# Strassen's algorithm for six more first-layer chunks, and a table that says which engine copies and adds

## The chip, the cores and the metric

The kernel runs on one core of one Trainium2 chip. The metric is device time in microseconds (us) for one execution; lower is better. Everything is float32, apart from the two weight matrices, which arrive as 64-bit floats and are turned into float32 on the chip. The core's engines are TensorE (PE in the profile; PEld is its loading of stationary operands), VectorE (DVE), ScalarE (ACT), GpSimd (POOL) and SyncE (SP, which only issues DMAs here).

## The reference

Eight batches of 512 tokens, each with eight heads of 64, read from and write to 32 state rows per head; the joined rows then go through a two-layer network with the ELU function between. Cut to what matters:

```python
scores = x @ state.T * scale;  a  = softmax(scores);  xread = a  @ state   # (8, 8, 512, 64)
scores2 = state @ x.T * scale; a2 = softmax(scores2); sread = a2 @ x       # (8, 8, 32, 64)
x = concat([xread, sread], axis=2)  ->  (8 * 544, 512)
h = x @ w_in                                       # (4352, 2048)
g = where(h > 0, h, exp(min(h, 0)) - 1)
out = g @ w_out                                    # (4352, 512)
```

## The kernel before, in words

**The first layer without its input.** For the 512 tokens of a batch, `x @ w_in` is `a @ (state @ w_in)`. So the kernel makes M = state @ w_in per batch (256 rows of heads and states, 2048 columns; `make_m`, L757), and the first layer is M.T @ a.T, with 256 as the length of the sum. M is made in eight pieces of 256 columns (hc 0 to 7), and a *chunk* c (0 to 3) is two pieces, 512 of the 2048 hidden columns. The state rows of all batches go through `states` (L1656) at the end.

**Two ways to do a chunk.** Batches 2 to 7 use `ffn1_chunk` (L1013): Strassen's algorithm in Winograd's form, which multiplies 2x2 blocks with seven products in place of eight. Its left sums s1, s2, s3, s4 of M come from `sum_m` (L846, four operations of 256 columns on GpSimd), its right sums t1 to t4 of a from `sum_a` (L855, four of 256 on VectorE). Three copies carry partial sums between PSUM banks, two additions with a PSUM operand finish the blocks, and `elu` (L963) turns each of the four blocks of 512 columns into g. Batches 0 and 1 use `ffn1_plain` (L982): per chunk four tiles, each two matmuls with a moving operand of 512 columns, and `elu`. An `elu` is Exp on ScalarE, then either Relu on ScalarE and one VectorE operation, or two VectorE operations.

**Order of stages.** `start` (L1302) loads x, the states and sixteen weight blocks of 1 MB each (three raw buffers, so block n+3 can be loaded only when block n has been converted). `convert` (L1255) is two ScalarE operations and four VectorE operations per block, the last of them an exact 32-bit integer addition that shows in the profile as CUSTOM_DVE_ANT_0. Blocks 0 to 7 are w_in, 8 to 15 w_out. In between it makes a and M of batches 0 and 1 and does their eight chunks; then follows their second layer (also Strassen, `Strassen` L1202 and `Second` L1067, whose sums are VectorE operations of 512 or 1024 columns). `batch` (L1573) then does batches 2 to 7, each prepared while the one before it is in its second layer.

**What sets the order.** No engine's order follows the program text. The kernel is written as 2,832 numbered operations; `Plan.add` (L290) finds their dependencies, and `ORDERS` (L50) holds for each engine the list of operation numbers in the order in which it issues them. `Plan.follow` (L364) walks these lists with a table of costs (for VectorE and GpSimd it takes a shared port as held by one of them at a time: `port`, L541 to L575) only to interleave the program and place 40 us of filling matmuls (`fill`, L1728) where TensorE would wait at the start. On the chip each engine runs its list strictly in order and waits on semaphores. SyncE's list sets the order of the loads. All engine instructions are issued from one helper, so the profile names them all L532.

Of the kernel before, what the change touches and what calls it, by code (L numbers as in the profile page):

```python
# [22 lines left out]
    "load_w": (0.46, 325e3), "load_x": (0.55, 297e3, 0.2), "load_states": (0.6, 180e3, 0.2),  # L23
    "load_blocks": (0.66, 280e3, 2.1), "move_state": (0.66, 280e3, 0.6),
# [16 lines left out]
def in_order(text):  # L41

    ops = []
    for part in text.split():
# [4 lines left out]

ORDERS = {  # L50
    PE: in_order(
        "26 23 16 29 89 92 201 19 203 95 69 59 66 205 81 85 127 63 62 138 134 217 215 130 112 116 157 142 146 178 "
        "160 171 182 186 190 174 248 245 226 230 259 262 219 222 234 266 278 270 282 305 308 320 317 286 290 324 "
        "410 411 423 294 442 443 336 274 332 424 412 348 444 340 413 425 414 445 446 426 352 328 427 344 428 415 "
        "447 416 417 451 452 448 453 429 430 480-482 491-494 483 449 495 484-486 500 487 496-498 528 454-456 "
        "529-532 541 533 534 542 623 535 543 544 550-552 545 457 553 546 554 458 555 547 548 556 557 628 571 570 "
        "629 619 573 574 639 620 621 640 625 641 643 645 648 649 665 662 663 685 609 670 671 667 682 683 693 687 "
        "661 694 697 709 743 706 707 746 712 681 780 747 752 767 754 745 783 784 759 808 789 782 812 811 791 796 "
        "817 832 810 819 835 836 824 841 834 887 843 848 864 870 860 903 871-873 892 893 884 885 883 900 901 889 "
        "989 905 908 973 899 909 978 970 979 971 986 975 969 987 1007 994 991 995 1035 1004 985 1005 1023 1009 "  # L60
        "1012 1013 1073 1020 1031 1003 1032 1021 1044 1025 1045 1019 1050 1076 1077 1097 1047 1082 1075 1110 1084 "
        "1089 1113 1114 1138 1119 1112 1141 1142 1121 1126 1147 1162 1140 1149 1165 1166 1154 1171 1164 1217 1173 "
        "1178 1194 1200 1190 1201 1319 1222 1223 1202 1230 1203 1213-1215 1231 1219 1233 1235 1238 1239 1229 1300 "
        "1301 1303 1305 1308 1309 1353 1316 1317 1299 1321 1337 1324 1325 1333 1315 1334 1335 1342 1343 1339 1350 "
        "1351 1403 1355 1365 1361 1362 1406 1407 1374 1375 1440 1380 1349 1377 1412 1405 1443 1414 1419 1444 1427 "
        "1449 1442 1468 1451 1456 1472 1471 1492 1470 1477 1495 1496 1479 1501 1484 1494 1503 1520 1508 1547 1649 "
        "1563 1532 1533 1552 1544 1545 1553 1549 1524 1530 1531 1543 1560 1568 1561 1569 1565 1630 1559 1633 1631 "
        "1638 1635 1639 1629 1654 1646 1655 1647 1664 1651 1695 1667 1645 1665 1733 1683 1669 1672 1673 1663 1691 "
        "1680 1692 1681 1679 1685 1770 1704 1705 1737 1710 1736 1707 1742 1735 1774 1773 1749 1744 1779 1757 1772 "
        "1798 1781 1786 1822 1801 1800 1802 1807 1825 1826 1809 1831 1814 1824 1833 1850 1877 1838 1854 1860 1862 "  # L70
        "1861 1863 1873 1874 1882 1875 1883 1893 1890 1891 1879 1889 1895 1898 1963 1899 1975 1968 1960 1969 1961 "
        "1976 1979 1965 1977 1959 1981 1984 2025 1985 1997 1994 1993 1995 2002 1999 2013 2003 2021 2010 2022 2011 "
        "2034 2015 2035 2063 2040 2009 2066 2087 2037 2100 2072 2067 2103 2074 2065 2104 2109 2079 2128 2102 2111 "
        "2152 2116 2131 2132 2155 2137 2156 2161 2139 2130 2163 2154 2180 2144 2168 2207 2192 2193 2191 2204 2205 "
        "2203 2212 2209 2213 2223 2220 2190 2184 2221 2219 2225 2228 2289 2293 2229 2298 2290 2299 2291 2306 2309 "
        "2295 2307 2327 2314 2311 2315 2305 2324 2343 2325 2355 2329 2379 2332 2323 2333 2351 2340 2352 2416 2341 "
        "2339 2364 2345 2365 2381 2370 2383 2382 2367 2388 2419 2420 2390 2395 2425 2403 2427 2418 2440 2442 2432 "
        "2443 2464 2444 2449 2467 2468 2451 2473 2456 2466 2513 2475 2480 2492 2494 2546 2562 2498 2509 2499 2518 "
        "2510 2519 2511 2529 2515 2497 2526 2525 2534 2527 2535 2531 2543 2542 2544 2558 2548 2551 2637 2552 2567 "
        "2559 2568 2560 2580 2564 2577 2596 2578 2585 2582 2667 2586 2604 2593 2665 2594 2605 2598 2608 2576 2635 "  # L80
        "2609 2592 2611 2639 2638 2669 2644 2668 2646 2674 2694 2676 2651 2750 2698 2681 2697 2751 2722 2703 2725 "
        "2696 2731 2724 2733 2705 2752 2759 2726 2753 2710 2754 2755 2760 2738 2756 2782 2757 2761 2762 2771 2763 "
        "2772 2764 2783 2784 2773 2774 2765 2775 2785 2776 2786 2777 2778 2787 2766 2792 2793 2788 2794 2795 2789 "
        "2796-2799 2812 2822 2813 2814 2802-2805 2815 2806-2809 2823 2824 2816-2819 2825-2829 "
    ),
    DVE: in_order(
        "28 25 18 48 30-32 54 36 195 194 35 50 49 55 39 56 51 57 41 21 42 44 43 200 122 45 123 97 124 96 125 102 "
        "98 84 208 209 105 101 152 107 110 108 111 109 154 153 88 155 168 115 166 137 167 169 145 119 240 242 141 "
        "241 243 181 185 149 256 254 255 214 257 300 193 477 302 301 189 229 303 312-315 225 358 360 269 233 237 "
        "359 478 365 361 281 366 273 367 368 537 289 285 372 374 373 297 375 386-389 327 379 419 335 381 380 382 "  # L90
        "277 395 420 393 339 407 394 405 406 293 396 351 408 399 434 421 343 331 401 400 436 422 716 720 476 438 "
        "402 435 479 437 439 538 355 440 432 441 489 502 501 507 433 503 490 347 518 517 562 506 717 510 512 516 "
        "539 431 536 514 603 576 652 582 655 578 579 565 586 583-585 540 604 632 581 549 563 580 566 577 567 633 "
        "653 564 636 631 568 459 569 656 606 654 637 638 626 657 635 627 674 658 646 651 723 659 675 678 647 634 "
        "523 679 718 660 680 673 668 676 719 677 669 721 688 690 689 696 691 605 713 714 750 751 722 755 758 762 "
        "807 763 787 788 765 792 806 766 815 799 816 800 795 858 802 820 803 804 879 823 828 840 805 844 827 831 "
        "881 852 851 847 856 857 877 875 876 917 878 855 859 933 922 880 897 882 916 895 913 896 918 891 906 932 "
        "907 914 982 898 925 911 915 981 921 998 927 983 976 977 931 929 984 912 943 992 961 944 997 999-1001 963 "
        "1002 938 993 962 1016 1010 1017 1015 964 1018 1011 1034 1026-1029 1051 1052 1080 1081 1085 1093 1088 "
        "1095 1117 1118 1096 1136 1092 1122 1137 1145 1146 1130 1125 1129 1188 1132 1133 1150 1135 1209 1153 1158 "  # L100
        "1170 1174 1157 1161 1134 1182 1177 1186 1205 1185 1206 1207 1246 1187 1208 1181 1210 1211 1189 1212 1227 "
        "1225 1247 1226 1243 1228 1252 1262 1248 1241 1263 1221 1255 1236 1244 1245 1312 1328 1251 1311 1242 1313 "
        "1257 1329 1306 1307 1322 1330 1259 1314 1268 1327 1331 1261 1291 1273 1274 1293 1323 1332 1237 1345 1346 "
        "1340 1292 1341 1348 1347 1356-1358 1294 1364 1359 1381 1382 1410 1411 1415 1422 1423 1425 1447 1418 1426 "
        "1448 1452 1459 1460 1455 1475 1462 1476 1463 1518 1539 1480 1541 1500 1488 1483 1504 1465 1487 1507 1512 "
        "1516 1517 1535 1491 1536 1467 1519 1466 1511 1515 1464 1540 1537 1542 1538 1555 1557 1556 1573 1551 1577 "
        "1576 1558 1575 1592 1582 1593 1566 1574 1642 1572 1643 1571 1636 1641 1578 1644 1637 1567 1585 1658 1581 "
        "1657 1587 1652 1653 1591 1589 1603 1604 1659-1661 1676 1670 1678 1677 1621 1662 1675 1622 1671 1598 1694 "
        "1624 1686-1689 1711 1712 1623 1740 1741 1745 1753 1752 1755 1756 1777 1778 1748 1797 1782 1790 1794 1785 "
        "1792 1789 1793 1795 1805 1848 1806 1869 1810 1796 1830 1813 1818 1867 1834 1817 1837 1821 1846 1847 1842 "  # L110
# [128 lines left out]
class Plan:  # L239
# [50 lines left out]
    def add(self, engine, cost, emit, ins, outs, port=False, moved=0, tokens=((), ()), name="", shape=None):  # L290
# [38 lines left out]
        for b in banks.values():  # L329
# [4 lines left out]
            b.last = op  # L334
        op.deps.discard(op)
        self.ops.append(op)
        return op

    def prepare(self):
        for op in self.ops:  # L340
# [114 lines left out]
def kernel(  # L455
# [340 lines left out]
    def copy_m(b, c, to):  # L796
        for g in range(G):
            A.copy(out=to[:, g * 512 : (g + 1) * 512], in_=st[b, "m", c][g])
# [974 lines left out]
```

## Time and profile before

| what | value |
|---|---|
| median of three runs (lowest, highest) | 688.26 us (687.98, 689.55) |
| the profiled execution: its time, its span | 688.75 us, 687.0 us |
| TensorE clock granted | full, in all 40 slices of the span |
| busy in the span: PE, DVE, ACT, POOL | 678.3, 568.5, 328.7, 110.2 us |
| TensorE: first matmul that is no filling, last matmul's end | 4.64 us, 683.3 us |
| start of the first matmul of batch 2's first layer | 186.07 us |

The page's first part gives busy time per engine, its second part the span in 40 slices of 17.2 us. Later views cut the span in stretches of one's own choice (busy time of each engine in each), group instructions by the tiles that they write and read and by shape (`out<-in`, count, busy time, mean ns of one), list who waited for whom, or show instructions in order of time. One float32 matmul of the program stands as two matmul records. A record's duration includes its way through the array and overlaps the next one, so the pace is read from a run of records in the timeline.

### The profile page before, as it was taken

To read this page: it belongs to the slowest core of one execution; us is meant where nothing else is said; L and a number is where in the kernel's file an instruction comes from. 1 tells how busy PE (TensorE), PEld (TensorE's weight loads), DVE (VectorE), ACT (ScalarE), POOL (GpSimd) and SP (SyncE) were. 2 spreads that over 40 slices of the span, in tenths; PEclk is the share of its full clock that TensorE was granted. 3 is DMA by queue.
4 is the path that set the end of the run, shared out by engine and by line. 5 is a ranking of instruction groups with operands and counts; after the bars stand their busy time and mean duration, and the time that the engine had idled before them with its cause. 6 is when DMAs were issued, how large, how long until landed. Compare 5 with 4: busy or idle time off the path is not lost.

```text
span 687.0 us, 15056 instructions
## 1 busy us (share of the span) xinstructions
PE 678.3 (99%) x6098; PEld 588.6 (86%) x6098; DVE 568.5 (83%) x896; ACT 328.7 (48%) x734; POOL 110.2 (16%) x133
## 2 busy tenths in 40 slices
PE   8999999999999999999999999999999999999997
PEld 7534568889988988899988998899889998999997
DVE  5999999989769993999569985998499966988661
ACT  5999972301266324833276316732484328611530
POOL 1100000200240124103230151112420333000000
PEclk9999999999999999999999999999999999999999
DMA  9899550007581046230573156213732040330401
GB/s 272 270 264 303 180 184 1 0 5 263 171 219 36 1 124 182 50 108 2 158 168 77 45 148 150 77 57 99 239 62 86 8 128 28 104 113 1 154 1 31
DMA packets 88457, 78.57 MB, mean 114 GB/s; under 512 B 56516, under 2 KB 69956, under 8 KB 88388
## 3 DMA queue, kind: packets, MB, share of 16 engines
q1 hardware_dynamic: 87844, 77.09, 38.4%
q8 instruction: 48, 0.79, 0.5%
q10 hardware_dynamic: 544, 0.52, 0.2%
q14 instruction: 21, 0.17, 0.1%
HBM read 59.77 MB, written 14.68 MB: 108 GB/s over the span
## 4 chain that ended last, share of the span: by engine, by line
PE 71%; issue 7%; ACT 6%; DMA 5%; DVE 5%; SPq 4%; POOL 1%; DVEq 0%; POOLq 0%
PE ps L532 71%; SPq L532 4%; ACT sec L532 3%; DMA xr<-in_state_dram 1%; DVE g L532 1%; POOL xr L532 1%; DMA o<-in_x_dram 1%; ACT t_w L532 1%; DVE xr L532 1%; DMA t_w<-in_moe_w_in_dram 1%; ACT w_half L532 1%; DMA m<-m_mem 1%; DVE sec L532 1%; DMA out_dram<-o 1%; ACT w_out L532 1%
## 5 line engine op out<-in xcount | busy, mean ns | idle before, releaser
L532 ACT COPY ps<-ps 128x128 f32<-128x128 f32 (+2 forms) x169 | 55.3, 332 | 227.6 <-PE ps L532 170.2
L532 PE MATMUL ps<-aT,m 128*128 128x256 f32 (+1 forms) x568 | 149.1, 406 | 1.1 <-DMA m<-m_mem 1.1
L532 PEld LDWEIGHTS ps<-aT,m 128*128 128x128 f32 x568 | 105.0, 190 | 29.4 <-issue 11.7
L532 PE MATMUL ps<-w_out,g 128*128 128x128 f32 (+1 forms) x768 | 115.4, 293 | 0.0
L532 PEld LDWEIGHTS ps<-w_out,g 128*128 128x128 f32 x768 | 102.1, 192 | 6.2 <-ACT m L532 1.7
L532 DVE TENSOR_TENSOR o<-o,ps 128x256 f32<-128x256 f32 (+2 forms) x108 | 55.9, 531 | 39.2 <-PE ps L532 34.3
L532 POOL TENSOR_TENSOR m<-m 128x256 f32<-128x256 f32 x72 | 56.9, 805 | 120.3 <-ACT m L532 103.9
L532 POOL TENSOR_TENSOR xr<-xr,small 128x512 f32<-128x512 f32 x24 | 31.0, 1305 | 278.0 <-PE ps L532 168.5
L532 PE MATMUL ps<-sec 128*128 128x128 f32 x560 | 72.9, 276 | 0.0
L532 PEld LDWEIGHTS ps<-sec 128*128 128x128 f32 x560 | 67.7, 192 | 1.0 <-issue 0.4
L532 PE MATMUL ps<-t_w,s 128*128 128x128 f32 (+1 forms) x432 | 67.9, 299 | 0.0
L532 ACT ACTIVATE xe<-ps 128x512 f32<-128x512 f32 x96 | 55.5, 597 | 14.4 <-PE ps L532 8.0
L532 PEld LDWEIGHTS ps<-t_w,s 128*128 128x128 f32 x432 | 59.0, 191 | 3.8 <-issue 0.8
L532 DVE SCALAR_TENSOR_TENSOR g<-xe,ps 128x512 f32<-128x512 f32 x66 | 43.9, 678 | 7.3 <-ACT xe L532 6.8
L532 DVE TENSOR_TENSOR ps<-sec,ps 128x512 f32<-128x512 f32 (+1 forms) x52 | 34.7, 668 | 9.7 <-PE ps L532 6.3
L532 ACT ACTIVATE xe<-xe 128x512 f32<-128x512 f32 x66 | 41.0, 633 | 1.1
L532 PE MATMUL ps<-aT,s 128*128 128x256 f32 x168 | 41.1, 379 | 0.2 <-DVE ps L532 0.2
L532 ACT COPY sec<-ps 128x512 f32<-128x512 f32 (+1 forms) x52 | 29.6, 569 | 21.2 <-PE ps L532 21.1
L532 ACT COPY m<-ps 128x256 f32<-128x256 f32 (+1 forms) x56 | 26.9, 497 | 26.6 <-PE ps L532 26.3
L532 PE MATMUL ps<-sec,g 128*128 128x128 f32 (+1 forms) x392 | 37.7, 259 | 1.2 <-DMA g<-in_x_dram 1.2
L532 PEld LDWEIGHTS ps<-sec,g 128*128 128x128 f32 (+1 forms) x392 | 34.7, 173 | 2.5 <-DMA g<-in_x_dram 1.7
L532 PE MATMUL ps<-w_out,sec 128*128 128x256 f32 (+1 forms) x176 | 36.6, 351 | 0.0
(149 smaller groups left out, 1158.0 us busy)
## 6 DMA issues: line engine op xcount, KB each, us to landing
w_half<-w_in_mem SPq DMA_DIRECT2D x48, 512.0 KB, 4.8
t_w<-in_moe_w_out_dram SPq DMA_DIRECT2D x8, 1024.0 KB, 5.6
t_w<-in_moe_w_in_dram SPq DMA_DIRECT2D x7, 1024.0 KB, 7.1
out_dram<-o SPq DMA_DIRECT2D x14, 512.0 KB, 4.2
xe<-in_x_dram SPq DMA_DIRECT2D x26, 256.0 KB, 3.2
o<-in_x_dram SPq DMA_DIRECT2D x80, 64.0 KB, 3.0
w_in_mem<-w_half SPq DMA_DIRECT2D x8, 512.0 KB, 3.8
xr<-xr SPq DMA_DIRECT2D x96, 32.0 KB, 3.0
```

Of the source, the lines that this page charges most:

```text
L532: ins = getattr(engine, name)(**named)
```

## The change

1. **Six chunks.** Chunks 1, 2 and 3 of batches 0 and 1 go through `ffn1_chunk`; chunk 0 of both stays plain. They get their own `sum_m` and, once per batch, `sum_a`; scratch space comes from buffers that are free at that time, and the third PSUM bank from the common pool.
2. **Places.** Copies, two-operand sums, the short scale operations and the middle step of `elu` go through `plan.pick`, which looks the operation's number up in a table `PLACES` of 110 entries; without an entry the engine is the one of before. Read with the numbering, the entries move, ahead of batch 2's first layer, 32 operations from DVE to POOL (ten additions of `convert`; seven `combine` halves of 1024 columns; seven sums of `sum_a` for batches 0 and 1; and some of 512 columns), 14 from POOL to DVE (13 of `sum_m`), 23 from ACT to DVE (13 of them copies of M of 256 columns) and 6 from DVE to ACT. From batch 2 on, 29 go from DVE to POOL and 6 others move.
3. **Orders.** All five lists are new. On SyncE the load of weight block 1 now stands ahead of batch 1's x; the states of batches 2 to 7 and block 2 follow. On TensorE the matmuls of batch 3's first chunk that stood six places (of 775) earlier against the work around them now come later.
4. **Costs in the table** for three kinds of DMA change and two are added; this moves only the plan's own times, not the orders, which are written out.

There are 2,912 operations after it: 775 on PE (757 before), 895 on DVE (896), 195 on POOL (126), 713 on ACT (719) and the same 334 on SP.

```diff
+    def pick(self, options, engine):
+        engine = PLACES.get(len(self.ops), engine)
+        options[engine]()
+        return engine
...
+    def both(out, in0, in1, op, engine=DVE):
+        plan.pick(
+            {
+                DVE: lambda: V.tensor_tensor(out=out, in0=in0, in1=in1, op=op),
+                POOL: lambda: Q.tensor_tensor(out=out, in0=in0, in1=in1, op=op),
+            },
+            engine,
+        )
...
-        V.tensor_tensor(out=bits, in0=bits, in1=q, op=ALU.add)
+        both(bits, bits, q, ALU.add)
...
-        pa, pc, pb = bank(), bank(), fixed[c % 2].view()
+        pa, pc, pb = bank(), bank(), bank() if b < 2 else fixed[c % 2].view()
+        u = ob[:, b * 1024 :] if b < 2 else sec[:, 7680 + c % 2 * 1024 :]
...
+        def ffn1_sums(b, c):
+            if (b, c) == (b, {0: 1, 1: 1}[b]):
+                sum_a((a_sb, s_buf)[b])
+            more = m1_more[c] if b else None
+            sum_m(g_of[b, c], more)
+            for part in ffn1_chunk(b, c, (g0, g_sb)[b], (a_sb, s_buf)[b], more):
+                part()
...
-            ffn1(0, c)
             if c < 2:
                 for b in range(2):
                     softmax_rows(b)
                     turn_state(b)
                     state_read(b, (x_halves, x_1)[b])
-            ffn1(1, c)
+            for b in range(2):
+                ffn1_sums(b, c)
```

## The prediction, made before the result was known

> **What bounds the kernel now.** I read four views in this order: the page's head, busy time by stage, TensorE's waits, and single stretches of the timeline.
>
> ```profile
> span 687.0 us, 15056 instructions
> PE 678.3 (99%) x6098; PEld 588.6 (86%) x6098; DVE 568.5 (83%) x896; ACT 328.7 (48%) x734; POOL 110.2 (16%) x133
> ```
>
> The stages (busy PE, PEld, DVE, ACT, POOL):
>
> ```profile
> 6.00:20.00 14.00, 12.32 (x300) 9.35 (x308) 12.25 (x24) 10.37 (x24) 2.16 (x2) 1.00 1.08 312
> 20.00:60.00 40.00, 39.65 (x493) 18.57 (x478) 37.50 (x54) 39.81 (x80) 2.06 (x2) 1.00 0.88 273
> 60.00:100.00 40.00, 39.77 (x181) 22.87 (x180) 39.23 (x49) 37.05 (x58) 0.00 (x0) 1.00 0.70 220
> 100.00:150.00 50.00, 50.00 (x238) 41.46 (x238) 45.69 (x57) 11.22 (x23) 4.96 (x4) 1.00 0.00 1
> 150.00:185.00 35.00, 35.00 (x332) 33.02 (x331) 34.69 (x59) 4.99 (x17) 1.82 (x3) 1.00 0.56 184
> ```
>
> TensorE's waits in the whole span:
>
> ```profile
> PE ps L532 <- DMA g<-in_x_dram: 1.2, 3, 0.7
> PE ps L532 <- DMA m<-m_mem: 1.1, 1, 1.1
> PE ps L532 <- ACT m L532: 0.5, 2, 0.3
> PE ps L532 <- DMA xr<-in_state_dram: 0.4, 1, 0.4
> ```
>
> A busy PE could still be a slow one, so the pace decides. From two runs of records:
>
> ```profile
> 70.89 3.70 PE L532 MATMUL ps<-s,g 128*128 128x512 f32 x8
> 87.32 1.89 PE L532 MATMUL ps<-w_out,sec 128*128 128x256 f32 x8
> ```
>
> Eight records of 512 columns take 3.70, and a single one stands with about 0.60 in the groups' mean, so they start every (3.70 - 0.60) / 7 = 0.44; where nothing waits, starts are 0.429 apart (0.10 of this run is its first record's). Likewise 256 columns start every 0.216. At these paces the gaps between full-size matmuls from 20 us to the end sum to some 9 us in 663, mostly pieces of 0.1 and less at changes of matmul shape; the largest is 1.3. So TensorE is the bound from 20 us to its last matmul at 683.3, and whatever leaves its list shortens the run, if the other engines still deliver in time. The stages show where that is doubtful: from 20 to 60 us DVE and ACT are at 94% and 99%, from 60 to 100 DVE at 98%, from 150 to 185 at 99%. The changed chunks lie between about 34 and 106 us.
>
> **TensorE's work: -4.9.** A plain chunk is 4 tiles x 2 matmuls x 2 records = 16 records of 512 columns, 16 x 0.429 = 6.86. By seven products it is 7 x 2 x 2 = 28 records of 256 columns, 28 x 0.216 = 6.05. The difference is 0.82; six chunks give 4.9. The weight loads (0.19 each) stay below 0.216 and hide.
>
> **What the chunks add elsewhere.** Per chunk: two PSUM additions on DVE (rows of 0.68 that start 0.61 apart), three PSUM copies of 0.58 (ACT), four sums of M of 256 columns; per batch four sums of a. That is 12 additions, 18 copies, 24 + 8 sums. The `elu` work has the same elements as before.
>
> **What the table moves, ahead of batch 2 (until 186 us).** DVE loses 32 operations to POOL and gets 14 from POOL, 23 from ACT (13 of 256 columns) and gives ACT 6. With starts 1.15 apart for 1024 columns, 0.61 for 512 and 0.35 for 256 I count, for operations that read two SBUF operands or run single-source in SBUF at double pace: before 54 x 1.15 + 30 x 0.61 + 56 x 0.61 + 8 x 0.35 = 117; after 38 x 1.15 + 30 x 0.61 + 49 x 0.61 + some 26 x 0.35 = 101. The other DVE operations grow from 94 to 124, about +15. DVE stays at 168 us, of some 175 (from 6 us to batch 2's start, 4 us earlier than now). ACT in its tight stage, 20 to 60, gives away nine copies and a few others and takes on the new PSUM copies of chunk 1: about 2.5 less, while TensorE saves 2 x 0.82 there. So the two tightest engines keep step. That is why I let the saving of TensorE stand. After batch 2's start DVE has 60 us of work in a batch of 83, so the 29 moves there I cost at nothing; what hides them is DVE's idle time (66.90 busy of 80 in 250 to 330); without it each would cost TensorE at most its extra length of some 0.4.
>
> **POOL's additions: +1.2.** POOL's rows:
>
> ```profile
> L532 POOL TENSOR_TENSOR m<-m 128x256 f32<-128x256 f32 x72 | 56.9, 805 | 120.3 <-ACT m L532 103.9 <-PE ps L532 9.9 <-DMA m<-m_mem 5.1
> L532 POOL TENSOR_TENSOR xr<-xr,small 128x512 f32<-128x512 f32 x24 | 31.0, 1305 | 278.0 <-PE ps L532 168.5 <-DVE small L532 78.3 <-issue 31.1
> ```
>
> Undisturbed ones take 0.72 (256) and 1.04 (512, one operand repeated). No row has 1024 columns or integers. From below, on the slope of these two: 0.72 + 3 x 0.32 = 1.7; from above, in proportion, 4 x 0.72 = 2.9. I take the middle, 2.3. As integers it might go as 2,048 half-words, as on DVE: 8 x 0.72 = 5.7, the far end. [...]
> DVE does the same addition in 1.15 steps, so a moved one comes 1.15 later. Four of them (blocks 1, 2, 3, 5) feed `make_m` from 20 to 60 us, and each is a new wait: PE's list is in order, so behind `make_m` stand all the ffn1 matmuls; behind the store of the block on SP stands the load of the next one. In the trace the time from the end of the last operation that feeds such a `make_m` to its start is 0.29, 0.23, 0.26 at three and about 2 at two. I charge one of four, 1.2. Ends: -0.7 (DVE earlier, TensorE's 0.7 of waits on M and the like gone) and +4.6 (all four).
>
> **Startup: +0.9.** With block 1 (1 MB) ahead of batch 1's x, x lands about 1 MB at 300 GB/s = 3.5 later than the 15.5 at which TensorE's last wait for it now ends, so near 19. By 19.95 TensorE now has behind it the state turns (0.7) and batch 1's scores (0.9) that it will then still owe, but it will have done 0.75 of `make_m`: 0.9 lost. Ends: 0 (filled by other work) and 1.6.
>
> **The fetch of M: -1.1.** TensorE waits 1.1 at 255.35 for a DMA issued at 249.74 behind SP's other issues. The new list uses it some six places (about 5 us) later. Ends: -1.3 and 0.
>
> **Sum**, against the profiled execution's 688.75: -4.9 + 1.2 + 0.9 - 1.1 = -3.9, so 684.8. Its time lies 0.49 above the median of 688.26; the median of the changed kernel should be **684.4**. The bounds added give -6.9 and +1.3: 681.4 to 689.6.
>
> **Rivals.**
>
> *The shared port eats the gain.* In one stretch (start, length):
>
> ```profile
> 255.45 3.15 POOL L532 TENSOR_TENSOR m<-m 128x256 f32<-128x256 f32 x3 [11.69 <-ACT m L532]
> 255.50 0.42 DVE L532 TENSOR_TENSOR aT<-aT 128x256 f32<-128x256 f32 x1
> 255.84 0.68 DVE L532 TENSOR_TENSOR g<-g 128x512 f32<-128x512 f32 x1
> ```
>
> Three POOL sums take 3.15 in place of 3 x 0.72 = 2.2 while DVE sums SBUF operands; elsewhere a DVE sum of 0.68 stands with up to 1.25 beside POOL. So they exclude each other. Then moving a sum to POOL frees DVE only for work that isn't of this kind. Ahead of batch 2: DVE 101 + POOL 72 (16 x 2.3 + 15 x 1.05 + 27 x 0.73) = 173 of 175 us. DVE's other work is only 67, so at least 5 of POOL's cannot lie beside it; each of POOL's 58 waits or makes wait by 0.3, as here, 17 in all: if half falls on DVE, it needs 168 + 9 = 177, 2 too many; if all, 185, 10 too many, of which 5 (weight sums that can wait until 210) can be put off. Price 2 to 5, I take 3.5: **687.9**. Against it: from 60 to 110 us the operands of TensorE's second-layer matmuls are 4 to 15 us ahead, far more than this lateness. Chance 0.15.
> [...]
>
> *Slower: POOL's integer addition.* If it takes the far end, 5.7, four additions ahead of `make_m` come 3.4 later each than I assume: 4 x 3.4 = 13.6, so **698**. It decides from the point where four times the excess passes 3.9, about 3.3 per addition. For it: no row of POOL has integers. Against: on DVE it runs at the float's pace (1.22 for 1024). Chance 0.09.
>
> *More gain.* ACT's relief and the earlier block 1 also remove the early waits: 688.26 - 4.9 - 1.1 - 0.7 = 681.5. Chance 0.10.
>
> **Numbers.** Forecast 0.66, the port 0.15, slower 0.09, more gain 0.10. Likeliest 684.4. Range 681.4 to 688.6: the lower bound of the costs, the port rival, and not the integer rival nor the last tail (under 0.2 together). About 0.2% (1.4 us) is what the measurement can tell from no change. Faster by more (below 686.9): 0.62 of the forecast's 0.66, the 0.10, and a third of the port's 0.15: 0.77. Within: 0.12. Slower: 0.09 and a tail of 0.02: 0.11.
>
> **What the new profile would show.** 32 records of 512-column matmuls in place of 128, and PE busy about 673.5. Batch 2's first first-layer matmul near 182.2 (now 186.07). POOL rows of 1024 at 1.7 to 2.9. TensorE's wait for m<-m_mem gone; one new wait of about 1 on POOL's w_half in 20 to 60 us. I am wrong if POOL's integer row is above 3.3, if TensorE waits on DVE by more than 3 ahead of 186 us, or if its first gapless stretch begins after 21.

## The result, and the profile after it

The changed kernel takes **694.0 us** (median of six runs, 691.67 to 695.92), the kernel before on the same chip 688.17 (six runs, 687.10 to 689.55): 1.0080 times as long, 95% interval 1.0057 to 1.0103. It is slower by 0.8%, where 684.4 was predicted and 688.6 was the upper end of the range. The profiled execution took 694.3 us, 5.55 more than that of before.

The head of the page:

```profile
span 692.4 us, 15404 instructions
PE 680.6 (98%) x6196; PEld 606.4 (88%) x6196; DVE 567.6 (82%) x895; ACT 331.4 (48%) x728; POOL 231.0 (33%) x202
```

TensorE's busy time grew by 2.3 us although it got less to do. Its list is now: 32 records of 512 columns in full-size products (128 before) and more of 256. At the paces of the prediction (0.429 and 0.216 us for 512 and 256 columns), with 0.112 for 128 (in before the 16 records from 655.28 take 1.79 to the next operation's start) and operations of smaller tiles at their least time in the profile of before, the whole list is worth 656.0 us, that of before 660.9. That is the predicted 4.9. So the question is where TensorE lost more than 4.9. I take as **lost** at a time t what lies between t and the worth of all that TensorE had done by then, filling apart:

| lost by (us) | before | after | added in the stretch |
|---|---|---|---|
| 20 | 10.1 | 12.1 | 2.0 |
| 35 | 11.9 | 17.7 | 3.8 |
| 190 | 15.2 | 24.5 | 3.5 |
| end | 22.2 | 32.5 | 1.0 |

10.3 more lost and 4.9 won make the 5.4 by which the profiled span grew. More than half of it comes before 35 us, where no chunk by Strassen's algorithm has begun. The stages of after (busy PE, PEld, DVE, ACT, POOL; granted clock, DMA share, GB/s):

```profile
6.00:20.00 14.00, 13.72 (x304) 11.50 (x296) 11.54 (x21) 8.87 (x18) 3.83 (x4) 1.00 1.10 314
20.00:60.00 40.00, 36.79 (x527) 20.77 (x527) 37.00 (x64) 35.36 (x72) 20.14 (x15) 0.96 0.75 250
60.00:100.00 40.00, 40.00 (x236) 32.65 (x235) 39.14 (x63) 38.10 (x63) 22.59 (x17) 1.00 0.56 182
100.00:150.00 50.00, 48.05 (x244) 40.16 (x243) 48.10 (x58) 16.19 (x28) 21.84 (x9) 1.00 0.48 129
```

Two things are new: from 20 to 60 us TensorE idles for 3.2 and its clock is 0.96, and from 100 to 150 it idles for 2 while VectorE is fuller than it was (48.10, before 45.69) in spite of 17 us more on GpSimd. TensorE's waits name both places:

```profile
PE ps L561 <- issue: 2.3, 1, 2.3
PE ps L561 <- POOL s L561: 1.6, 1, 1.6
...
PE ps L561 <- DVE sec L561: 0.8, 2, 0.7
PE ps L561 <- POOL w_half L561: 0.7, 1, 0.7
```

The first has no releaser: "issue" means that no semaphore in the profile explains it. The timeline of TensorE around it:

```profile
24.84 2.80 PE L561 MATMUL ps<-w_half,kT 64*32 64x256 f32 x96
27.57 0.97 PE L561 MATMUL ps<-xe,xr 128*32 128x64 f32 x50
30.84 0.42 PE L561 MATMUL ps<-xe,xr 128*32 128x64 f32 x14 [2.30 <-issue]
31.19 5.40 PE L561 MATMUL ps<-aT,m 128*128 128x512 f32 x8
```

TensorE stops at 28.54 in the middle of one operation (batch 0's state read, 64 records, of which 50 are done) and goes on 2.3 us later. Then eight records of 512 columns take 5.40 in place of 3.70, because the granted clock is 0.5 from 31.39 to 34.80: four records start 0.855 apart in place of 0.429, 1.7 us more. In six executions of this kernel the clock averaged 1.000 in the two shortest (691.67, 692.40), 0.998 in the three longest (694.3 to 695.92).

### The profile page after: what moved, and what is told of

Same layout as the page of the kernel before. It is cut to its first block, busy times and chain, and to the rows that moved or that the text cites. A ratio compares the mean times of both kernels' runs of the same rounds, so it can differ in the third digit from the quotient of the medians.

```text
span 692.4 us, 15404 instructions
## 1 busy us (share of the span) xinstructions
PE 680.6 (98%) x6196; PEld 606.4 (88%) x6196; DVE 567.6 (82%) x895; ACT 331.4 (48%) x728; POOL 231.0 (33%) x202
## 4 chain that ended last, share of the span: by engine, by line
PE 82%; DVE 8%; ACT 3%; DMA 2%; SPq 2%; POOL 1%; issue 1%; DVEq 0%; ACTq 0%; POOLq 0%
PE ps L561 82%; SPq L561 2%; DMA t_w<-in_moe_w_in_dram 2%; DVE g L561 1%; DVE sec L561 1%; DVE w_out L561 1%; DVE t_w L561 1%; ACT xe L561 1%; DVE xr L561 1%; DVE ps L561 1%; ACT t_w L561 1%; DMA xe<-in_x_dram 0%; POOL s L561 0%; POOL w_half L561 0%; ACT sec L561 0%
## 5 line engine op out<-in xcount | busy, mean ns | idle before, releaser
L561 ACT COPY ps<-ps 128x128 f32<-128x128 f32 (+2 forms) x174 | 58.2, 339 | 198.8 <-PE ps L561 152.5
L561 PEld LDWEIGHTS ps<-aT,m 128*128 128x128 f32 x604 | 112.3, 191 | 22.3 <-issue 6.5
L561 POOL TENSOR_TENSOR m<-m 128x256 f32<-128x256 f32 x80 | 68.8, 876 | 59.6 <-ACT m L561 46.5
L561 ACT ACTIVATE xe<-ps 128x512 f32<-128x512 f32 x120 | 69.6, 597 | 24.5 <-DVE ps L561 12.2
L561 DVE SCALAR_TENSOR_TENSOR g<-xe,ps 128x512 f32<-128x512 f32 x76 | 50.6, 679 | 11.7 <-ACT xe L561 11.2
L561 ACT ACTIVATE xe<-xe 128x512 f32<-128x512 f32 x86 | 53.0, 632 | 1.3
L561 POOL TENSOR_TENSOR s<-s 128x256 f32<-128x256 f32 x27 | 21.4, 803 | 61.9 <-ACT s L561 57.5
L561 ACT COPY m<-ps 128x512 f32<-128x512 f32 (+1 forms) x48 | 23.0, 501 | 32.1 <-PE ps L561 31.3
```

Of the source, the lines that this page charges most:

```text
L561: ins = getattr(engine, name)(**named)
```

## The experiments

Each kernel was run beside the kernel before on the same chip; the chips differ, so ratios to before are what is compared. Where "the lists were put in order again", single operations were moved up and down in the lists of ORDERS by the plan's own costs until its end no longer came earlier.

| kernel | median, us | before beside it | ratio (95%) |
|---|---|---|---|
| after | 694.0 | 688.17 | 1.0080 (1.0057 to 1.0103) |
| e1 state read behind two tiles | 691.19 | 689.37 | 1.0025 (1.0010 to 1.0040) |
| e2 one sum back on VectorE | 699.16 | 689.37 | 1.0136 (1.0113 to 1.0159) |
| e3 x of batch 1 loaded first | 695.63 | 689.37 | 1.0080 (1.0063 to 1.0097) |
| e4 no table ahead of batch 2 | 693.73 | 689.37 | 1.0061 (1.0040 to 1.0082) |
| e5 e1, no table from 195 us on | 688.35 | 688.51 | 1.0000 (0.9987 to 1.0012) |
| e6 start of before | 694.64 | 688.51 | 1.0094 (1.0074 to 1.0115) |
| e7 chunks without the table | 690.84 | 688.51 | 1.0039 (1.0027 to 1.0051) |
| e8 block 4 loaded later | 694.48 | 688.51 | 1.0086 (1.0073 to 1.0099) |
| e9 stores of w_in later as well | 700.33 | 689.20 | a single execution |
| e10 e5, put in order again | 689.44 | 689.20 | 1.0005 (0.9994 to 1.0017) |
| e11 e5, four additions on VectorE | 691.70 | 689.20 | 1.0041 (1.0026 to 1.0055) |
| e12 e10, a wait filled | 690.62 | 688.50 | 1.0026 (1.0007 to 1.0045) |

And what TensorE lost in them, in the profiled executions, by time:

| lost by (us) | before | after | e1 | e4 | e5 | e7 | e11 |
|---|---|---|---|---|---|---|---|
| 20 | 10.1 | 12.1 | 13.0 | 12.5 | 12.1 | 12.7 | 12.2 |
| 35 | 11.9 | 17.7 | 13.6 | 13.7 | 12.9 | 16.1 | 14.1 |
| 60 | 13.5 | 19.7 | 16.2 | 18.3 | 15.5 | 19.8 | 20.4 |
| 100 | 14.4 | 21.2 | 17.6 | 20.8 | 16.9 | 23.2 | 21.9 |
| 190 | 15.2 | 24.5 | 20.4 | 23.1 | 19.1 | 23.7 | 24.0 |
| end | 22.2 | 32.5 | 29.5 | 32.0 | 25.9 | 29.8 | 30.7 |

**The stop at 28.5 us: e1, e8, e9.** My theory after reading the two traces: TensorE ran out of instructions, and the clock fell because of it. The page counts the packets that carry them:

```profile
q8 instruction: 49, 0.80, 0.5%
```

49 packets of 16 KB stand against 12,392 matmul and weight-load records, 253 a packet, so I take it that this queue feeds TensorE. The packet that begins at 28.29 ends at 29.27, and TensorE goes on 1.6 us later.

Where TensorE stops says the same. Counted from the start of the trace, filling included, TensorE has done 1,217 records when it stops in after (1,212 of matmuls and weight loads, 5 others), and just as many in e2, e3 and e8, although these stops begin at other times (28.24 to 30.93 us) and the one of e3 comes behind 24 records of the state read in place of 50. In e7 it has done 961, which is 256 fewer, close to the 253 that come to one packet. So the stops go by the number of records done, about a packet's worth apart, and not by what some operation lacks of its own.

```diff
@@ TensorE's list (189 is the state read, 81 and 134 are tiles) @@
-63 189 81 134 138 85
+63 81 134 189 138 85
@@ ScalarE's list @@
-68 190 100 165 82 191
+68 100 165 82 190 191
```

> The changed kernel with one operation of TensorE moved: the state read of batch 0, in which TensorE stood from 28.54 to 30.84 us, comes behind the first two tiles of chunk 0, and ScalarE's scaling of its result behind the Exp of the first tile. Theory (one stop): TensorE's instructions ran out, after a stretch of some 330 small matmuls, because a 16 KB fetch of instructions came late; the clock then fell to half for 3.4 us. With two long tiles (3.4 us for 16 instruction records each) in between, the fetch is there in time: no gap above 1 us, the clock full in all runs, 694.0 - 2.3 - 1.7 = 690.0. Rival: the state read waits for something of its own (its data, a bank), the gap moves with it, and the time stays at 694 within 0.7.

Measured: 691.19, ratio 1.0025, so 0.55% (3.8 us) less than after; the stop is gone and the clock of the profiled execution is full (in one of the twelve, 694.57, it averaged 0.996). The timeline of e1:

```profile
27.47 3.70 PE L566 MATMUL ps<-aT,m 128*128 128x512 f32 x8
31.10 1.10 PE L566 MATMUL ps<-xe,xr 128*32 128x64 f32 x64
32.13 3.70 PE L566 MATMUL ps<-aT,m 128*128 128x512 f32 x8
```

The same operation now runs its 64 records without a break, and the tiles on both sides of it take 3.70. The packet still begins at 28.26, as late as in after: TensorE has long tiles to do until it is there. The rival is out. Why was the packet late?

```diff
@@ SyncE's list in e8 (58 loads block 3, 126 block 4; 78 and 131 store w_in, 74 stores M) @@
-58 78 131 126 74 161
+58 78 131 74 126 161
@@ the same in e9 @@
-58 78 131 126 74 161
+58 74 126 78 131 161
```

> The changed kernel with one number of SyncE's list moved: the load of weight block 4 (1 MB, issued at 22.74 us) comes behind the first store of M (issued at 30.43). TensorE's lists stay, with all small matmuls in one stretch. Theory: the 16 KB packet of instructions that TensorE ran out for came late (28.29 us) because the DMA engines were 90% busy from 20 to 29 us with 3 MB issued between 20.2 and 23.3; with 1 MB less ahead of it the packet comes up to 3 us earlier, TensorE does not stop, the clock stays full, and the time is 690.0. Rival: the stretch of small matmuls outruns the fetch whatever the traffic; the gap of 2.3 stays, and the time is 694.

Measured: 694.48, ratio 1.0086; the packet begins at 28.17 and the stop stays, at the same record:

```profile
27.29 0.97 PE L566 MATMUL ps<-xe,xr 128*32 128x64 f32 x50
30.56 0.65 PE L566 MATMUL ps<-xe,xr 128*32 128x64 f32 x14 [2.30 <-issue]
```

So the load of block 4 had nothing to do with it, and the theory as I had put it fell. But in e8 the DMA engines were still busy until some 27.9 us with what had been issued before 22.4. If the packet waits its turn, only what was issued *before* it was asked for matters; that is block 3 and the two stores, 2 MB.

> The changed kernel with three numbers of SyncE's list moved: the load of weight block 4 and the two stores of converted w_in (0.5 MB each, issued at 20.62 and 22.29 us) come behind the first store of M (30.43). It costs time behind 31 us, since buffers come free later (some 7 us); only the stretch up to 31 us is asked about. In e8 the load alone was moved and the instruction packet still came at 28.17, but there the DMA engines stayed busy until 27.5 with what had been issued before 22.7. Theory (the packet queues behind what was issued before it was asked for): with 1 MB less ahead of it, it comes by 25 us and TensorE does not stop in the state read. Rival (the stretch of small matmuls outruns the fetch whatever the traffic): the packet comes near 28 and the gap of 2.3 to 2.5 us stays.

Measured (one execution, 700.33; a loss behind 31 us was expected from the buffers that come free later): the packet begins at 25.34, and TensorE does not stop. It has done 961 records at 24.68, 0.7 us ahead of the packet's start, and 1,217 at 27.91, 2.6 us behind it; in after it has done 961 at 25.11, and the packet begins only 3.2 us later. The timeline of e9, then the DMA queues from 20 to 29 us in after and in e9 (packets, MB, share of 16 engines):

```profile
27.14 1.20 PE L566 MATMUL ps<-xe,xr 128*32 128x64 f32 x64
28.27 5.42 PE L566 MATMUL ps<-aT,m 128*128 128x512 f32 x12
```

```profile
q1 hardware_dynamic: 1092, 2.63, 89.9%
```

```profile
q1 hardware_dynamic: 688, 1.34, 45.8%
```

e8 and e9 have TensorE's lists unchanged, small matmuls in one stretch and all; only traffic differs. So in these runs the stop took both: a stretch in which TensorE takes instructions fast (318 records of small matmuls, each with its weight load, in the 10 us ahead of the stop), and data transfers issued ahead of the packet. Before has less of both: its SyncE issued nothing between 14.8 and 22.25 us, and behind 224 such records in 8 us its first tile begins at 23.51.

**The load order: e3, e6.**

```diff
@@ SyncE's list (10 is weight block 1, 11 to 14 batch 1's x) @@
-0-2 10 14 13 12 11 8
+0-2 14 13 12 11 10 8
```

> The changed kernel with the load of weight block 1 put back behind batch 1's x on SyncE, as before, and nothing else. It tells what the load order alone is worth with all other lists as they are. By the prediction's own term (0.9 for x coming late) the time would fall by 0.9 to 693.1. By the trace: the turns of x end 2 to 3 us earlier, but TensorE's list has the second piece of M ahead of all first-layer tiles, and block 1 is converted 3.5 us later, so TensorE stands at that piece from 22 to about 25.8: 2.0 saved and 3.5 lost, 695.5, if the stop at 28.5 stays; if the pause lets the instruction fetch catch up, 4.0 less, 691.5.

Measured: 695.63, ratio 1.0080, no better than after. TensorE in e3:

```profile
13.05 1.16 PE L566 MATMUL ps<-sec,g 64*64 64x64 f32 x64
...
20.74 0.66 PE L566 MATMUL ps<-sec,sec 128*128 128x128 f32 x4 [0.31 <-ACT sec L566]
...
25.14 1.10 PE L566 MATMUL ps<-w_half,kT 64*32 64x256 f32 x32 [0.59 <-POOL w_half L566]
```

In after these three begin at 16.30, 17.40 and 22.32. So the first turn of x comes 3.3 earlier, but the operation behind it 3.3 later, because ScalarE's list has the conversion of block 1 ahead of what releases it, and block 1 now reaches ScalarE at 17.61 in place of 14.14. The piece of M from block 1 is 2.8 late. The stop stayed, 1.94 long, with the clock full behind it. Alone the load order is worth nothing; the other lists are made for it. With the whole start of before (12 entries of the table fewer):

> The changed kernel with the first 30 us of before (its load order with batch 1's x ahead of weight block 1, its places and lists), and the lists behind it put in order again up to 190 us; six chunks by Strassen's algorithm and the rest of the table stay. Theory: the 2.0 us that TensorE loses by 20 us because x comes late go, and with pieces of M and tiles taking turns the small matmuls do not run dry of instructions: 694.0 - 4.1 - 2.0 = 688, a little under before. Rival: block 1 is converted 4 us later, the lists behind 30 us were made for the earlier piece, and the 2 us come back as waits on ScalarE and VectorE between 35 and 60 us: 690 to 691, as e1.

Measured: 694.64, ratio 1.0094. The rival held, and by more than it said: lost by 20 us 10.5, by 35 13.9, without a stop; but 23.4 by 190, 9.5 in that stretch, of which 2.4 are one wait for a GpSimd addition (w_out). These lists behind 30 us are one arrangement among many, so this shows that the late x was part of a bargain (block 1 earlier), not that the bargain was the best.

**GpSimd's sums: e2, e4, e7, e11.** In after, the longest wait behind GpSimd looks like this (start, length):

```profile
139.10 1.21 DVE L561 TENSOR_TENSOR t_w<-w_out,t_w 128x1024 f32<-128x1024 f32 x1
139.32 3.20 POOL L561 TENSOR_TENSOR s<-s,sec 128x1024 f32<-128x1024 f32 x1 [1.34 <-DVE sec L561]
...
140.83 2.24 DVE L561 TENSOR_TENSOR sec<-g 128x512 f32<-128x512 f32 x1
...
142.58 3.72 PE L561 MATMUL ps<-t_w,s 128*128 128x256 f32 x16 [1.62 <-POOL s L561]
```

GpSimd's sum, 2.37 undisturbed, is held up until VectorE's of 139.10 is done; then VectorE's next sum of two SBUF operands, 0.68 elsewhere, stands until GpSimd's has ended. Summed over all VectorE operations that start ahead of 185 us, what they take beyond the shorter ones of their shape (the lower fifth in the profile of after) is 11.4 us, in before 2.3; on GpSimd 12.3, in before 1.5. The durations of these VectorE operations add up to 188.3 us, in before to 185.8: 32 operations had gone to GpSimd, but 37 came from GpSimd and ScalarE, and 12 additions of the chunks.

```diff
@@ VectorE's list (570 is the sum at 139.32) @@
-513 520 539
+513 570 520 539
@@ GpSimd's list @@
-658 570 619
+658 619
@@ GpSimd's entries in PLACES @@
-518 521 570 619
+518 521 619
```

> The changed kernel with one addition of 1024 columns (the second half of s+a11 of batch 0, 3.20 us on GpSimd at 139.32, for which TensorE stands 1.6 us at 142.58) put back on VectorE, right behind the operation that it waits for. Theory: it ends near 140.4, ahead of its use at 141, and VectorE does not get longer by its 1.15, since its sum of 2.24 us at 140.83 was itself held up by that GpSimd sum: 694.0 - 2.0 = 692.0, with the start as it is. Rival (VectorE is the bound there, busy 48.1 of 50 us from 100 to 150): the 1.15 shows up a few operations later as a wait on VectorE, and the time is 693.5 or more.

Measured: 699.16, ratio 1.0136. The rival held, and by far more than it said: put back, the sum makes VectorE so late that TensorE stands 3.9 us for it at 149, after which the clock halves for 3.4 us. Part of this is GpSimd again: its next sum now begins 4.9 us earlier, and beside it VectorE's sum takes 3.38 in place of the 1.21 of 139.10 above. In e2:

```profile
137.59 3.12 POOL L566 TENSOR_TENSOR s<-g 128x1024 f32<-128x1024 f32 x1 [1.61 <-PE ps L566]
...
138.42 3.38 DVE L566 TENSOR_TENSOR t_w<-w_out,t_w 128x1024 f32<-128x1024 f32 x1
...
149.13 2.07 PE L566 MATMUL ps<-w_out,sec 128*128 128x256 f32 x4 [3.93 <-DVE m L566]
```

From 137.28 us to the end of what TensorE waits for, no idle time of VectorE is listed: it is the bound there. Without the whole early part of the table:

> The changed kernel without the 72 entries of the table ahead of batch 2 (ten conversion additions, the combine halves and sums of a back on VectorE, sums of M back on GpSimd, copies back on ScalarE), the lists put in order again for that; six chunks by Strassen's algorithm and the load order stay. If the moves to GpSimd are what costs (the shared port), the time falls: of the 10.2 us lost only the 5.8 of the first 35 us stay, 688.2 - 4.9 + 5.8 = 689. If the moves are needed because VectorE would otherwise be the bound (its work ahead of batch 2 is then 168 + 12 additions of 0.61 + 8 sums of 0.35 = 178 of 175 us, with no room for its own waits of 8 to 10), VectorE is late by 8 to 12 and the time is 695 to 700.

Measured: 693.73, ratio 1.0061, between the two. e4 has no stop (its state read stands behind tiles), so it is to be read against e1: 0.36% or 2.5 us slower, all of it by 190 us (23.1 lost against 20.4). VectorE's lengthening ahead of 185 us is 2.6 in e4, 10.9 in e1, and its durations add up to the same, 190.6 and 190.5. So waiting beside GpSimd takes its toll, and the 72 early entries as a whole are still worth 2.5. They relieve ScalarE too (busy 40.00 of 40 us from 20 to 60 in e4, 39.37 in e1); which engine's relief it is, e4 doesn't show.

> Six chunks by Strassen's algorithm without the table (one entry of 110 is left), the lists put in order again; weight block 1 still ahead of batch 1's x. It is e4 with the late part of before as well. If the late moves cost 2.0: 693.7 - 2.0 = 691.7. If they cost nothing: 693.7. If VectorE needed the table throughout, more than 694.

Measured: 690.84, ratio 1.0039, of which 1.73 us is a stop for instructions of its own at 24.9. It comes nearest to the reading by which the late moves cost 2.0. Without the stop it would stand at about 689, so the chunks with the new load order, but without the moves, win nothing: TensorE has 4.9 less to do, and loses 5.9 more in waiting (29.8 - 22.2, less 1.7). Of these 2.6 lie ahead of 20 us, where there is no chunk; from 35 to 190 us, where the chunks are, e7 loses 7.6 and before 3.3. Against e5, which has the same late part, e7 is 2.7 us slower, 1.0 without the stop: less than the 2.5 of e4 against e1.

The edit, on e5 (the four numbers also leave GpSimd's list and PLACES):

```diff
@@ VectorE's list @@
-124 123 57
+124 123 125 57
-153 154 97
+153 154 155 97
-168 167 136
+168 167 169 136
-288 287 88
+288 287 289 88
```

> The kernel of e5 with the four early conversion additions (weight blocks 1, 2, 3 and 5, 2.35 to 2.69 us each on GpSimd, 1.22 on VectorE) back on VectorE, each right behind its last operand. By the prediction's term (they come 1.15 late on GpSimd, one of four uncovered, 1.2) the time falls to 687.1. By the other reading (VectorE is the bound from 30 to 60 us, and the moves relieve it by 4 x 1.2): TensorE is late by up to 4 us by 60 us, 690 to 692.

Measured: 691.70, ratio 1.0041 against 1.0000 of e5: the four additions are worth 2.8 us on GpSimd. The profiled execution (692.34) loses, beside that, 1.7 us at half clock from 40.3 us on, which the median one (691.70, clock 1.000) has not; it stands behind this wait:

```profile
PE ps L565 <- DVE sec L565: 1.8, 2, 1.3
```

**The moves from batch 2 on: e5.** The edit takes 37 entries, from some 195 us on, out of PLACES, and the lists of before take their place there.

> The kernel of e1 (state read of batch 0 behind two tiles) with the places and lists of before from about 195 us on (37 of the table's entries gone, most of them moves of 1024 and 512 columns to GpSimd). In the trace of e1 TensorE loses 9.1 us from 185 us to the end, in that of before 7.1. Theory: the late moves cost these 2.0 (VectorE's operations are 19 us longer in all than undisturbed ones from 185 on, 9 in before), so the time falls from 691.2 to 689.2. Rival, the prediction's own step (29 late moves cost nothing, since VectorE has idle time): 691.2 within 0.7.

Measured: 688.35, ratio 1.0000, 0.25% or 1.7 us less than e1: the theory held. TensorE loses 6.8 from 190 us on, in e1 9.1, in before 7.1. Busy times from 185 to 684 us (PE, PEld, DVE, ACT, POOL) in e1, then in e5:

```profile
185.00:684.00 499.00, 496.85 (x4489) 458.17 (x4488) 393.37 (x635) 224.63 (x528) 148.57 (x143) 1.00 0.33 92
```

```profile
185.00:684.00 499.00, 495.67 (x4490) 457.19 (x4489) 404.33 (x664) 222.45 (x529) 100.70 (x119) 1.00 0.32 92
```

48 us of GpSimd's time relieve VectorE by 11, in a stretch where VectorE idles for a fifth. Of the 2.3 us, 0.9 is a wait of e1 for a DMA (at 343 us) that after does not have. The largest of the other waits that e5 lacks is one for VectorE, 0.66 at 538.08 in after: VectorE's sum ahead of it took 1.52 in place of 0.68 beside a sum on GpSimd. e5 takes back places and orders together, so it does not part the two.

**A faster version: e10, e12.** e5 is as fast as before. Two attempts to get under it:

> The kernel of e5 (table ahead of batch 2 only, state read behind two tiles) with the same table and loads, and its lists for the stretch from 36 to 200 us put in order again with GpSimd's measured prices (2.37 for 1024 columns, 1.27 for 512 of two operands) in place of lower ones. In e5 TensorE still loses 3.4 us between 35 and 150, before 2.7, and in the start 12.9 against 11.9. If what is left between 35 and 150 us is order, 1 to 2 us go: 686.5 to 687.5, which would be faster than both kernels. If it is bound by VectorE's and GpSimd's work as a whole: 688.3.

Measured: 689.44, ratio 1.0005: no gain. It loses 1.0 from 60 to 130 us (e5: 2.6) and then a wait of 1.3 at 131.27 (listed as "issue"; VectorE's sum that TensorE needs ends at that moment) and others give it back by 150 (19.3, e5 19.0). Order is not what is left.

```diff
@@ TensorE's list, on e10 @@
-577 608 578 609 580 689 621
+577 578 689 608 609 580 621
```

> The kernel of e10 with two operations of TensorE moved ahead of the one that stands 1.34 us at 131.27 for VectorE's sum s+a11 of batch 0 (ended 131.17): a product of 1 us whose operands are ready, and the piece of M of batch 2. If TensorE's time there is only a matter of order, 1.3 us go: 688.1, some 0.15% under before. If the products that now come behind are late in turn for the sums behind that one, which VectorE and GpSimd make one after the other, the wait comes back within 15 us: 689.4.

Measured: 690.62, ratio 1.0026, twelve executions from 687.43 to 694.34. In the profiled one (694.25) TensorE waits 3.2 for VectorE (m) behind 140 us, and the clock is half from 149.2 to 152.6: the wait came back, longer. No version tried beats the kernel before.

## Why the prediction was wrong, step by step

- **TensorE's work, -4.9: right.** 660.9 to 656.0, and the 32 records of 512 columns are there. Batch 2's first first-layer matmul, foretold for 182.2, starts at 190.44 (before 186.07): 4.4 later, which is the 9.3 more that TensorE has lost by then less the 4.9. Busy time (680.6, 673.5 foretold) was a poor sign: an engine at half clock counts as busy (in after 3.41 of the 3.41 us from 31.39), and so does one between two shapes (before is busy for 85.00 of the 85 us from 100 to 185, and loses 0.8 from 100 to 190).
- **Startup, +0.9: the step that failed.** Its own term, x coming late, measured 2.0 by 20 us (its end was 1.6). But it took for granted that TensorE, once it has operands, gets on at full clock. The reordered list puts all small matmuls behind one another while 2 MB of weight traffic stands ahead of their instructions: 2.3 us of stop and 1.7 of half clock, 4.0 in all, which e1 took away (3.8) by moving one operation of TensorE and one of ScalarE. I had named "its first gapless stretch begins after 21" as a sign that I am wrong; it begins at 31.2. No row of before showed such a stop, and the prediction bounded only the late x.
- **GpSimd's additions, +1.2: the price right, the sign wrong.** The rows of after:

```profile
L561 POOL TENSOR_TENSOR s<-g 128x1024 f32<-128x1024 f32 x5 | 12.3, 2454 | 15.0 <-DVE g L561 14.9
L561 POOL TENSOR_TENSOR w_half<-w_half,t_w 128x1024 uint32<-128x1024 uint32 x5 | 12.1, 2427 | 15.1 <-DVE w_half L561 5.6 <-ACT o L561 3.4 <-DVE t_w L561 3.4
L561 POOL TENSOR_TENSOR w_out<-w_out,t_w 128x1024 uint32<-128x1024 uint32 x4 | 10.6, 2662 | 13.7 <-ACT xe L561 8.9 <-DVE t_w L561 4.8
```

  2.4 to 2.7 against 2.3, integers like floats, so the rival at 5.7 is out. The one new wait is there (w_half, 0.7 at 22.3). But e11 shows, on e5's lists, that the same four additions on VectorE cost 2.8: VectorE's relief was worth more than the lateness, and I had counted only the lateness.
- **"The two tightest engines keep step": wrong, and this was the rival of the shared port.** From 35 to 190 us TensorE loses 6.8, before 3.3: 3.5, the price that the rival gave. VectorE's operations grew by the 9 us that it worked out for half of the waits. No run shows a port as such; what they show is that sums of the two engines lengthen each other (VectorE's of 0.68 to 2.24, GpSimd's of 2.37 to 3.20 at 139 us). That the price came out to the tenth is luck, since it was the middle chosen between 2 and 5, and no run parts what this lengthening costs from what the chunks' own additions cost. What the rival did not see: without the moves this stretch is worse (9.4 lost in e4, 7.6 in e7). I argue, but have not shown, that this is because the chunks put 12 additions and 8 sums on a VectorE that was full. I gave the rival 0.15 on the ground that operands of the second layer are 4 to 15 us ahead from 60 to 110 us. There TensorE has indeed no wait listed; 2.5 of the 3.5 are paid behind 100 us, at 118 to 149, where TensorE's products wait in a row for sums that VectorE and GpSimd make one after another.
- **The fetch of M, -1.1: right.** From 240 to 280 us TensorE loses 0.6, before 1.7, and the wait is no longer listed.
- **29 late moves at nothing: wrong by 2.** e5, which takes back the late orders as well, won 1.7 in time and 2.3 in what TensorE lost from 190 us on. VectorE's idle time, on which I had counted, does not hide a wait where the sum that TensorE reads next is held up beside GpSimd, as at 538 us.

Added up by the runs: -4.9 (work), +2.0 (x late), +3.8 (stop and half clock 4.0, the rest of that stretch 0.2 less than before), +3.5 (chunks' sums and the lengthening beside GpSimd, not parted), +1.0 (late moves and orders +2.1, M -1.1) make +5.4, which is the span's growth. What stays open: what exactly makes the clock halve, how the 3.5 divides, and whether another arrangement of the same operations beats the kernel before; e6, e10 and e12 are only three.

## What to carry to other kernels

A saving on the engine that sets the time is kept only if the engines beside it have room where it is made: count what the new algorithm puts on them in that stretch, with what they lengthen each other by (here 9.1 us more on VectorE and 10.8 more on GpSimd ahead of 185 us). Moving an operation to a slower engine helped here where the faster one was full (e11), and did not help where it idled for a fifth of the time (e5), however idle the slower one was. When the order of a start is changed, look at the instruction stream as well as at the data: here 318 records of small matmuls in 10 us, with 2 MB of transfers issued ahead of an instruction packet, came before a stop of 2.3 us.

## What the runs showed of the hardware that I had not expected

- **TensorE's instruction packet came later with more data issued ahead of it.** With 2 MB ahead the 16 KB packet began at 28.29 (after) and 28.17 us (e8), with 1 MB at 25.34 (e9), with the same instructions on TensorE. In five kernels (after, e2, e3, e7, e8) TensorE stopped for 1.7 to 2.4 us and went on 2.35 to 2.55 us after the packet's start, at whatever time that was (24.26 to 30.52), and always after 961 or 1,217 records.
- **The clock halved behind some short stops, for 3.41 us.** It was 0.5 for 3.41 us after 2.3 us of stop (after, e8) and after a wait of 1.3 among small matmuls (e11); after stops of 1.9 and 2.4 (e3, e2) it stayed full. In the traces of after and before the stretches of full and half clock last whole multiples of 3.413 us (23.89, seven of them, then 3.41 in after; 682.67, 200 of them, in before). Set out in pieces of that length by an estimate of mine, 2.30 us of the stop of after and 2.13 of that of e8 lie within one piece, and the next piece is at half clock; the stop of e2 is split by the end of a piece at 29.66 into 1.42 and 0.95, and at most 1.82 of that of e3 lies in one piece. So where a stop falls seems to matter, and not only its length; but idle time in one piece doesn't decide it either, since in e11 the half clock came behind a piece with 1.59 idle.
- **A sum on GpSimd held one on VectorE until it had ended** (0.68 became 2.24 at 140.83), which the prediction had from a row of before; new is the total of what their operations take beyond the shorter ones of their shape: 11.4 us on VectorE and 12.3 on GpSimd in 185 us, 2.3 and 1.5 before.
